# A Winograd 3x3 convolution: shorter prologue and epilogue by finer semaphores and merged weight loads

## The chip, the cores and the metric

The kernel runs on one core of a Trainium2 chip. The metric is the device time of one execution in microseconds (us), as the median of several runs. The profile adds one traced execution, whose span (first to last instruction) is 528.9 us.

## The reference

The reference is a 3x3 convolution with padding 1 over a 512 x 512 image with 96 channels in and 96 out, in bf16, written as Winograd F(2x2, 3x3):

```python
U = jnp.einsum("ar,rsck,bs->abck", G, w, G)            # transformed weights
xp = jnp.pad(x, ((0,0),(1,1),(1,1),(0,0)))
# d: all 4x4 patches of xp, two pixels apart
V = jnp.einsum("ai,ijpc,bj->abpc", Bt, d, Bt)          # transformed input
M = jnp.einsum("abck,abpc->abpk", U, V)                # products
Y = jnp.einsum("ma,abpk,nb->pmnk", At, M, At)          # back: 2x2 outputs a patch
```

The kernel uses the Winograd form along the rows only. For each pair of output rows (2t, 2t+1) it makes four combinations of input rows (a = 0 to 3), multiplies each with transformed weights, and recombines the four products into two output rows. Along the columns it keeps three taps.

## The kernel before

There are T = 256 row pairs. For each pair t:

- SyncE loads two rows of x with a transposing DMA into a ring of 8 buffers (`Xn`), so that channels lie on partitions.
- VectorE makes the four transforms of the rows (`Vt`, ring of 8).
- TensorE makes products 1 and 2 in two PSUM banks ("first half-step", 12 matmuls), and later adds products 0 and 3 into the same banks ("second half-step", 12 matmuls, `finish_pair`).
- ScalarE evacuates both banks after each half-step (one instruction of 128 x 768 for both banks), into `Ms`.
- VectorE makes the two output rows from the four evacuated tiles (`compute_y`), and GpSimd stores four rows at a time; SyncE stores the last four in two stores.

The weights, nine tiles of 96 x 96, are loaded by nine DMAs, three on each of three issuers:

```python
def load_weight(eng, sem, r, s_):
    src = bass.AP(w.tensor, w.offset + (r * 3 + s_) * C * K, [[K, C], [1, K]])
    off = r * KB + (2 - s_) * K
    eng.dma_start(Wraw[0:C, off:off + K], src).then_inc(sem, 16)

w_split = {
    "sp": [(1, 0), (1, 1), (1, 2)],
    "act": [(0, 0), (0, 1), (0, 2)],
    "pool": [(2, 0), (2, 1), (2, 2)],
}
```

```python
@block.sync
def _(sp):
    wt = _Waiter(sp)
    for (r, s_) in w_split["sp"]:
        load_weight(sp, w_sems["sp"], r, s_)
    for m in range(T):
        load_pair(sp, wt, m)              # L158: transposing load of rows 2m, 2m+1
    out_dma_pair(sp, wt, T - 2, o_last)   # L198, waits for y_cnt
    out_dma_pair(sp, wt, T - 1, o_last)
    sp.wait_ge(o_last, 32)
```

VectorE clears its borders and a tile of zeros, waits for all weights, transforms them, and then begins with x. Pairs 0 and 1 are transformed one by one (`v_single`), later pairs two at a time (`v_ops`, one instruction for two pairs):

```python
# vector engine
wait_weights(wt)
W0, W1, W2 = ...                          # rows of the 3x3 kernel, 96 x 288 each
dve.tensor_tensor(Wf1[0:C, :], W0, W2, ALU.add).then_inc(u_sem, 1)            # L325
dve.tensor_single_scalar(Wall[0:C, 0:KB], W0, 2.0, ALU.mult)
dve.tensor_single_scalar(Wall[0:C, 3 * KB:4 * KB], W2, 2.0, ALU.mult)
wt("u", u_sem, 1)
dve.tensor_tensor(Wall[0:C, 1 * KB:2 * KB], Wf1[0:C, :], W1, ALU.add)         # L329
dve.tensor_tensor(Wall[0:C, 2 * KB:3 * KB], Wf1[0:C, :], W1, ALU.subtract).then_inc(u_sem, 1)
wt("init", init_sem, 1)
compute_vgroup_part(0, 0)                 # pair 0: four v_single, L261
compute_vgroup_part(0, 1)                 # pair 1
compute_vgroup_part(1, 0)                 # pairs 2 and 3: v_ops, L279
compute_vgroup_part(1, 1)
for t in range(T):
    compute_vgroup_part(t // 2 + 2, t % 2)
    if t >= 2:
        compute_y(t - 2)                  # L318, L319
compute_y(T - 2)
compute_y(T - 1)
```

TensorE fills the time before the first data with 16 matmuls on zeros (L361):

```python
# tensor engine
wt("init", init_sem, 1)
for i in range(N_WARM):                   # 16
    pe.matmul(psets[RPS - 1][:, BANK:2 * BANK], Zt[0:C, 0:Q], Zt[0:C, 0:BANK], start=True, stop=True)
wt("u", u_sem, 2)
wait_weights(wt)
...
for t in range(T):
    conv_set(t, 1, 0, False, waits=[("vd", v_dve, vd_target(t))])    # 6 matmuls, L381
    conv_set(t, 2, 1, False).then_inc(m12_done, 1)                   # 6 matmuls
    if t >= 1:
        finish_pair(t - 1)                                           # products 0 and 3, L378
finish_pair(T - 1)
```

```python
# scalar engine
def b_evacuate(tp):
    wt("ab", ab_done, tp + 1)
    act.activation(ms2_ap(tp, 2), banks2(tp), ACT.Copy, scale=0.5).then_inc(b_evac, 1)   # L233
```

Of the kernel before, what the change touches and what calls it, by code (L numbers as in the profile page):

```python
# [5 lines left out]
ACT = mybir.ActivationFunctionType  # L6
ALU = mybir.AluOpType
# [17 lines left out]
def bass_standalone__winograd__vision_kernel(  # L25
# [23 lines left out]
    RY = 16  # L49
# [4 lines left out]
    with ExitStack() as es, nc.Block() as block:  # L54
# [25 lines left out]
        o_last = es.enter_context(nc.semaphore("o_last"))  # L80

# [51 lines left out]
        def vd_target(t):  # L133
            if t == 0:
                return 1
            return 2 * (t // 2 + 1)
# [31 lines left out]
        def load_weight(eng, sem, r, s_):  # L168
            src = bass.AP(w.tensor, w.offset + (r * 3 + s_) * C * K, [[K, C], [1, K]])
            off = r * KB + (2 - s_) * K  # L170
            eng.dma_start(Wraw[0:C, off:off + K], src).then_inc(sem, 16)  # L171

        w_split = {
            "sp": [(1, 0), (1, 1), (1, 2)],
            "act": [(0, 0), (0, 1), (0, 2)],
            "pool": [(2, 0), (2, 1), (2, 2)],
# [15 lines left out]
        def out_dma_pair(eng, wt, t, sem):  # L192
            wt("yc", y_cnt, t + 1)
            yslot = (2 * t) % RY
            src = bass.AP(YO, yslot * KY, [[RY * KY, 128], [1, 2 * KY]])
            dst = bass.AP(out.tensor, out.offset + 2 * t * orow_elems,
                          [[KY, Q], [orow_elems, 2], [1, KY]])
            eng.dma_start(dst, src).then_inc(sem, 16)  # L198
# [3 lines left out]
        @block.sync  # L202
        def _(sp):
            wt = _Waiter(sp)
            for (r, s_) in w_split["sp"]:
                load_weight(sp, w_sems["sp"], r, s_)
            for m in range(T):
                load_pair(sp, wt, m)
            out_dma_pair(sp, wt, T - 2, o_last)
            out_dma_pair(sp, wt, T - 1, o_last)  # L210
            sp.wait_ge(o_last, 32)

        @block.gpsimd
        def _(pool):
            wt = _Waiter(pool)
            for (r, s_) in w_split["pool"]:
                load_weight(pool, w_sems["pool"], r, s_)
            ng_count = [0] * NG
            for g in range(NG_POOL):
                out_dma(pool, wt, g, o_dma[g % NG])  # L220
                ng_count[g % NG] += 1
            for sg in range(NG):
                pool.wait_ge(o_dma[sg], 16 * ng_count[sg])

        @block.scalar
        def _(act):
            wt = _Waiter(act)
            for (r, s_) in w_split["act"]:
                load_weight(act, w_sems["act"], r, s_)

            def b_evacuate(tp):
                wt("ab", ab_done, tp + 1)
                act.activation(ms2_ap(tp, 2), banks2(tp), ACT.Copy, scale=0.5).then_inc(b_evac, 1)  # L233

            for t in range(T):
                wt("m12", m12_done, t + 1)
                if t >= RM:
                    wt("yc", y_cnt, t - RM + 1)
                act.activation(ms2_ap(t, 0), banks2(t), ACT.Copy, scale=0.5).then_inc(m_evac, 1)  # L239
                if t >= 1:  # L240
                    b_evacuate(t - 1)
            b_evacuate(T - 1)

        @block.vector
        def _(dve):
# [45 lines left out]
            def compute_vgroup_part(g, which):  # L291
                if g >= NGRP:
                    return
                if g == 0:
                    if which == 0:
                        for a in (1, 2, 0):
                            v_single(0, a)
                        v_single(0, 3).then_inc(v_dve, 1)
                    else:
                        for a in (1, 2, 0):  # L300
                            v_single(1, a)
                        v_single(1, 3).then_inc(v_dve, 1)
                    return
# [9 lines left out]
            def compute_y(t):  # L313
                wt("be", b_evac, t + 1)
# [3 lines left out]
                dve.tensor_tensor(yo_ap(h0), ms_ap(t, 2), ms_ap(t, 1), ALU.add)  # L318
                dve.tensor_tensor(yo_ap(h0 + 1), ms_ap(t, 0), ms_ap(t, 3), ALU.subtract).then_inc(y_cnt, 1)  # L319

            wait_weights(wt)
            W0 = Wraw[0:C, 0:KB]
            W1 = Wraw[0:C, KB:2 * KB]
            W2 = Wraw[0:C, 2 * KB:3 * KB]
            dve.tensor_tensor(Wf1[0:C, :], W0, W2, ALU.add).then_inc(u_sem, 1)  # L325
            dve.tensor_single_scalar(Wall[0:C, 0:KB], W0, 2.0, ALU.mult)
            dve.tensor_single_scalar(Wall[0:C, 3 * KB:4 * KB], W2, 2.0, ALU.mult)
            wt("u", u_sem, 1)
            dve.tensor_tensor(Wall[0:C, 1 * KB:2 * KB], Wf1[0:C, :], W1, ALU.add)  # L329
            dve.tensor_tensor(Wall[0:C, 2 * KB:3 * KB], Wf1[0:C, :], W1, ALU.subtract).then_inc(u_sem, 1)  # L330
            wt("init", init_sem, 1)
            compute_vgroup_part(0, 0)
            compute_vgroup_part(0, 1)
# [22 lines left out]
        def _(pe):  # L356
# [7 lines left out]
            wait_weights(wt)  # L364
# [19 lines left out]
            def finish_pair(tp):  # L384
                conv_set(tp, 0, 0, True, waits=[("me", m_evac, tp + 1)])
                conv_set(tp, 3, 1, True,
                         waits=[("be", b_evac, tp + 2 - RPS + 1)]).then_inc(ab_done, 1)

            assert RPS >= 3
            for t in range(T):  # L390
                conv_set(t, 1, 0, False, waits=[("vd", v_dve, vd_target(t))])
# [32 lines left out]
```

## Time and profile before

| | before |
|---|---|
| median of 6 runs | 528.38 us |
| lowest and highest | 523.74 and 539.83 us |
| span of the traced execution | 528.9 us |
| granted clock of TensorE, mean | 0.99 |
| first matmul on real data | 9.25 us |
| last matmul over | 525.0 us |

In the profile's names, PE is TensorE, DVE is VectorE, ACT is ScalarE, POOL is GpSimd and SP is SyncE; SPq is SyncE's sequencer, which issues DMAs. L158 is line 158 of the kernel. A timeline row has its start, its duration, the engine and line, what is written and read, how many instructions were merged into the row, and in brackets how long the engine stood idle before it and what released it. A row of the groups of instructions ends with the time busy, the mean duration in ns and the idle time before it. Two instructions of VectorE can overlap a little at their ends, so the distance between starts says more than the duration.

### The profile page before, as it was taken

What the parts mean: (1) busy time and instruction counts of PE and PEld (TensorE: products, weight loads), DVE (VectorE), ACT (ScalarE), POOL (GpSimd) and SP (SyncE); (2) the same over time, 40 slices, a digit from 0 to 9 for tenths busy, and PEclk for the clock granted to TensorE, in tenths of its full rate; (3) what the DMA queues carried; (4) which work ended last, traced back from release to release, by engine and by line L of the source; (5) the groups of instructions that cost most, each with busy time, mean ns of one, the idle gap of its engine ahead of it and who ended that gap; (6) DMA issues with size and microseconds to landing.
All of it is one profiled execution on the core that took longest, in us unless ns stands there. A gap on an engine that the chain in (4) does not pass through costs nothing.

```text
span 528.9 us, 14957 instructions
## 1 busy us (share of the span) xinstructions
PE 519.4 (98%) x6160; PEld 496.7 (94%) x6160; DVE 468.2 (89%) x1099; ACT 415.2 (79%) x513; POOL 97.6 (18%) x134
## 2 busy tenths in 40 slices
PE   7999999999999999999998999999999999999997
PEld 3999999999999999999998899999999999999996
DVE  5899999999999999998786889979998999999992
ACT  2688888888888888888886688878888888888886
POOL 1112112112112112121121121212121212112111
PEclk8899999999999999999999899999999999999999
DMA  7999999999999999999999999999999999999963
GB/s 141 182 258 232 214 272 239 234 233 235 225 225 230 251 207 223 236 221 232 209 180 185 246 235 255 207 218 252 253 218 248 258 257 201 251 258 232 230 164 120
DMA packets 287476, 118.60 MB, mean 224 GB/s; under 512 B 274656, under 2 KB 277248, under 8 KB 287408
## 3 DMA queue, kind: packets, MB, share of 16 engines
q1 hardware_dynamic: 272752, 67.59, 82.5%
q0 software_dynamic: 14320, 50.00, 28.8%
q8 instruction: 48, 0.79, 0.6%
q14 instruction: 20, 0.16, 0.1%
q10 hardware_dynamic: 336, 0.06, 0.1%
HBM read 0.17 MB, written 50.33 MB: 95 GB/s over the span
## 4 chain that ended last, share of the span: by engine, by line
PE 82%; DMA 10%; DVE 3%; SPq 3%; issue 1%; ACT 0%; POOL 0%; DVEq 0%; ACTq 0%; POOLq 0%
PE ps L378 41%; PE ps L381 41%; DMA Xn<-in_x_dram 9%; SPq L158 3%; DVE Vt L279 1%; DMA Wraw<-in_w_dram 1%; DVE Vt L261 1%; ACT Ms L233 0%; DVE YO L318 0%; DVE Vt L282 0%; DVE YO L319 0%; POOL Wraw L171 0%; ACT Ms L239 0%; DVE Wf L325 0%; DVE Wall L330 0%
## 5 line engine op out<-in xcount | busy, mean ns | idle before, releaser
L279 DVE TENSOR_TENSOR Vt<-Xn 96x1024 bf16<-96x1024 bf16 x445 | 288.7, 680 | 26.1 <-DMA Xn<-in_x_dram 25.8
L381 PE MATMUL ps<-Wall,Vt 96*128 96x96 bf16 (+2 forms) x3072 | 298.4, 248 | 3.6 <-DVE Vt L279 2.1
L378 PE MATMUL ps<-Wall,Vt 96*128 96x96 bf16 (+2 forms) x3072 | 297.7, 247 | 0.5 <-ACT Ms L239 0.5
L381 PEld LDWEIGHTS ps<-Wall,Vt 96*128 96x128 bf16 x3072 | 247.8, 115 | 13.2 <-DVE Vt L279 2.6
L239 ACT ACTIVATE Ms<-ps 128x768 bf16<-128x768 f32 x256 | 207.5, 810 | 62.4 <-PE ps L381 54.0
L378 PEld LDWEIGHTS ps<-Wall,Vt 96*128 96x128 bf16 x3072 | 246.7, 115 | 9.7 <-ACT Ms L239 1.2
L233 ACT ACTIVATE Ms<-ps 128x768 bf16<-128x768 f32 x256 | 207.3, 810 | 46.1 <-PE ps L378 46.0
L190 POOL DMA_DIRECT2D out_dram<-YO x127 | 95.7, 753 | 425.8 <-DVE YO L319 410.2
L318 DVE TENSOR_TENSOR YO<-Ms 128x384 bf16<-128x384 bf16 x256 | 90.3, 353 | 24.9 <-ACT Ms L233 19.8
L319 DVE TENSOR_TENSOR YO<-Ms 128x384 bf16<-128x384 bf16 x256 | 89.2, 349 | 0.0
L282 DVE TENSOR_TENSOR Vt<-Xn 96x512 bf16<-96x512 bf16 x125 | 46.9, 414 | 1.4 <-DMA Xn<-in_x_dram 1.2
L361 PE MATMUL ps<-Zt 96*128 96x512 bf16 x16 | 6.4, 588 | 1.5 <-DVE Zt L249 1.5
L361 PEld LDWEIGHTS ps<-Zt 96*128 96x128 bf16 x16 | 2.2, 142 | 5.1 <-issue 3.6
L325 DVE TENSOR_TENSOR Wf<-Wraw 96x288 f32<-96x288 bf16 x1 | 0.5, 455 | 4.9 <-DMA Wraw<-in_w_dram 4.9
L239 ACT ACT_TABLE_LOAD x1 | 1.3, 1283 | 2.1 <-issue 2.1
L261 DVE TENSOR_TENSOR Vt<-Xn 96x512 bf16<-96x512 bf16 x7 | 2.5, 411 | 0.0
L171 POOL DMA_DIRECT2D Wraw<-in_w_dram x3 | 1.7, 573 | 0.9 <-POOLq L409 0.9
L247 DVE MEMSET Vt<- 128x32 bf16 x1 | 0.1, 85 | 0.9 <-PEq L409 0.9
L330 DVE TENSOR_TENSOR Wall<-Wf,Wraw 96x288 bf16<-96x288 f32 x1 | 0.4, 448 | 0.0
L329 DVE TENSOR_TENSOR Wall<-Wf,Wraw 96x288 bf16<-96x288 f32 x1 | 0.4, 447 | 0.0
L261 DVE TENSOR_TENSOR Vt<-Zt,Xn 96x512 bf16<-96x512 bf16 x1 | 0.4, 412 | 0.0
L282 DVE TENSOR_TENSOR Vt<-Xn,Zt 96x512 bf16<-96x512 bf16 x1 | 0.4, 412 | 0.0
(8 smaller groups left out, 1.2 us busy)
## 6 DMA issues: line engine op xcount, KB each, us to landing
out_dram<-YO POOLq DMA_DIRECT2D x127, 384.0 KB, 4.9
Xn<-in_x_dram SPq DMA_TRANSPOSE x256, 5.4
out_dram<-YO SPq DMA_DIRECT2D x2, 192.0 KB, 2.0
Wraw<-in_w_dram ACTq DMA_DIRECT2D x3, 18.0 KB, 2.3
Wraw<-in_w_dram SPq DMA_DIRECT2D x3, 18.0 KB, 2.1
Wraw<-in_w_dram POOLq DMA_DIRECT2D x3, 18.0 KB, 2.8
Xn<-in_x_dram SPq DMA_DIRECT2D x1, 3.0 KB, 4.8
```

Source lines behind the costliest of these rows:

```text
L158: eng.dma_start_transpose(xpair_ap(m, 0, 2 * W), src).then_inc(x_ld[ps], 16)
L190: eng.dma_start(dst, src).then_inc(sem, 16)
L233: act.activation(ms2_ap(tp, 2), banks2(tp), ACT.Copy, scale=0.5).then_inc(b_evac, 1)
L239: act.activation(ms2_ap(t, 0), banks2(t), ACT.Copy, scale=0.5).then_inc(m_evac, 1)
L261: return dve.tensor_tensor(vtile_ap(t, a, XC0, C, 1, W), xrow_ap(r0, C), xrow_ap(r1, C), op)
L279: res.append(dve.tensor_tensor(o, in0, in1, op))
L282: res.append(dve.tensor_tensor(vtile_ap(tt, a, XC0, C, 1, W), xrow_ap(r0, C), xrow_ap(r1, C), op))
L318: dve.tensor_tensor(yo_ap(h0), ms_ap(t, 2), ms_ap(t, 1), ALU.add)
L319: dve.tensor_tensor(yo_ap(h0 + 1), ms_ap(t, 0), ms_ap(t, 3), ALU.subtract).then_inc(y_cnt, 1)
L361: pe.matmul(psets[RPS - 1][:, BANK:2 * BANK], Zt[0:C, 0:Q], Zt[0:C, 0:BANK], start=True, stop=True)
L378: ins = pe.matmul(o, lhsT, rhs, start=False, stop=(idx == n - 1), skip_group_check=True)
L381: ins = pe.matmul(o, lhsT, rhs, start=(idx == 0), stop=(idx == n - 1))
```

## The change

The change is meant to shorten both ends of the pipeline.

- Weights: three DMAs instead of nine, each with one row of the 3x3 kernel (96 x 288). ScalarE issues two and GpSimd one. SyncE issues none, and so begins with x at once. The tiles now lie in plain order, and the reversal of the column taps moves into the weight operations, which become 96 wide.
- VectorE first makes three transforms of pair 0, then waits for the weights, makes the weights of products 1 and 2, then those of 0 and 3, and then the fourth transform of pair 0 and pair 1.
- TensorE may begin pair 0 when three of its transforms and the weights of products 1 and 2 are there.
- Pairs 2 to 5 are transformed one by one, each with its own signal, instead of two at a time.
- At the end the evacuation of the last pair is split by bank, each output row of the last pair has its own signal, and the last four rows go out in three stores instead of two.

The core of the diff (declarations of three semaphores and helper definitions are cut):

```diff
-        def vd_target(t):
+        NEARLY = 6
+        def vd_target(t, full=True):
             if t == 0:
-                return 1
-            return 2 * (t // 2 + 1)
+                return 2 if full else 1
+            if t < NEARLY:
+                return t + 2
+            return NEARLY + 1 + 2 * ((t - NEARLY) // 2 + 1)
...
-        def load_weight(eng, sem, r, s_):
...
+        def load_weight(eng, sem, r):
+            src = bass.AP(w.tensor, w.offset + r * 3 * C * K, [[K, C], [C * K, 3], [1, K]])
+            dst = bass.AP(Wraw, r * KB, [[3 * KB, C], [K, 3], [1, K]])
+            eng.dma_start(dst, src).then_inc(sem, 16)
         w_split = {
-            "sp": [(1, 0), (1, 1), (1, 2)],
-            "act": [(0, 0), (0, 1), (0, 2)],
-            "pool": [(2, 0), (2, 1), (2, 2)],
+            "sp": [],
+            "act": [0, 1],
+            "pool": [2],
         }
...
         # sync engine, end
-            out_dma_pair(sp, wt, T - 2, o_last)
-            out_dma_pair(sp, wt, T - 1, o_last)
-            sp.wait_ge(o_last, 32)
+            wt("yc", y_cnt, T - 1)
+            out_dma_rows(sp, H - 4, 2, o_last)
+            wt("y0l", y0_last, 1)
+            out_dma_rows(sp, H - 2, 1, o_last)
+            wt("yc", y_cnt, T)
+            out_dma_rows(sp, H - 1, 1, o_last)
+            sp.wait_ge(o_last, 48)
...
         # scalar engine
             def b_evacuate(tp):
+                if tp == T - 1:
+                    wt("al", a_last, 1)
+                    act.activation(ms_ap(tp, 2), bank(tp, 0), ACT.Copy, scale=0.5).then_inc(ae_last, 1)
+                    wt("ab", ab_done, tp + 1)
+                    act.activation(ms_ap(tp, 3), bank(tp, 1), ACT.Copy, scale=0.5).then_inc(b_evac, 1)
+                    return
...
         # vector engine, compute_vgroup_part
                     if which == 0:
-                        for a in (1, 2, 0):
-                            v_single(0, a)
+                        v_single(0, 1)
+                        v_single(0, 2)
+                        v_single(0, 0).then_inc(v_dve, 1)
+                    else:
                         v_single(0, 3).then_inc(v_dve, 1)
-                    else:
                         for a in (1, 2, 0):
                             v_single(1, a)
                         v_single(1, 3).then_inc(v_dve, 1)
+                    return
+                if 2 * g < NEARLY:
+                    tt = 2 * g + which
+                    if which == 0:
+                        wait_vslots(g)
+                    for a in (1, 2, 0):
+                        v_single(tt, a)
+                    v_single(tt, 3).then_inc(v_dve, 1)
                     return
...
         # vector engine, weights
-            wait_weights(wt)
...
-            dve.tensor_tensor(Wf1[0:C, :], W0, W2, ALU.add).then_inc(u_sem, 1)
-            dve.tensor_single_scalar(Wall[0:C, 0:KB], W0, 2.0, ALU.mult)
-            dve.tensor_single_scalar(Wall[0:C, 3 * KB:4 * KB], W2, 2.0, ALU.mult)
-            wt("u", u_sem, 1)
-            dve.tensor_tensor(Wall[0:C, 1 * KB:2 * KB], Wf1[0:C, :], W1, ALU.add)
-            dve.tensor_tensor(Wall[0:C, 2 * KB:3 * KB], Wf1[0:C, :], W1, ALU.subtract).then_inc(u_sem, 1)
             wt("init", init_sem, 1)
             compute_vgroup_part(0, 0)
+            wait_weights(wt)
...
+            dve.tensor_tensor(Wf1[0:C, :], wraw(0), wraw(2), ALU.add).then_inc(u_sem, 1)
+            wt("u", u_sem, 1)
+            ins = None
+            for s_ in range(3):
+                dve.tensor_tensor(wall(1, s_), wf1(s_), wraw(1, s_), ALU.add)
+                ins = dve.tensor_tensor(wall(2, s_), wf1(s_), wraw(1, s_), ALU.subtract)
+            ins.then_inc(u_sem, 1)
+            for s_ in range(3):
+                dve.tensor_single_scalar(wall(0, s_), wraw(0, s_), 2.0, ALU.mult)
+                ins = dve.tensor_single_scalar(wall(3, s_), wraw(2, s_), 2.0, ALU.mult)
+            ins.then_inc(u_sem, 1)
             compute_vgroup_part(0, 1)
...
         # tensor engine
             wt("u", u_sem, 2)
-            wait_weights(wt)
...
             def finish_pair(tp):
-                conv_set(tp, 0, 0, True, waits=[("me", m_evac, tp + 1)])
+                ins0 = conv_set(tp, 0, 0, True, waits=[("me", m_evac, tp + 1), ("vd", v_dve, vd_target(tp)),
+                                                    ("u", u_sem, 3)])
+                if tp == T - 1:
+                    ins0.then_inc(a_last, 1)
...
             for t in range(T):
-                conv_set(t, 1, 0, False, waits=[("vd", v_dve, vd_target(t))])
+                conv_set(t, 1, 0, False, waits=[("vd", v_dve, vd_target(t, full=False))])
```

## The prediction

> **What bounds the kernel now.** I read the page from the top: the busy shares, the 40 slices and the groups of instructions.
>
> ```profile
> PE 519.4 (98%) x6160; PEld 496.7 (94%) x6160; DVE 468.2 (89%) x1099; ACT 415.2 (79%) x513; POOL 97.6 (18%) x134
> ...
> L279 DVE TENSOR_TENSOR Vt<-Xn 96x1024 bf16<-96x1024 bf16 x445 | 288.7, 680 | 26.1 <-DMA Xn<-in_x_dram 25.8
> ...
> L325 DVE TENSOR_TENSOR Wf<-Wraw 96x288 f32<-96x288 bf16 x1 | 0.5, 455 | 4.9 <-DMA Wraw<-in_w_dram 4.9
> ```
>
> TensorE is busy nearly always; VectorE's longest idle stretches are waits for loads of x. Next comes the chain of waits, in order of time. Here it crosses from the start into the regular rhythm:
>
> ```profile
> 10.50 2.11 PE ps L381 x12
> 12.61 1.92 PE ps L378 x12
> 14.53 1.92 PE ps L381 x12
> 16.45 1.46 PE ps L378 x12
> 17.91 0.99 PE ps L381 x12
> ```
>
> One half-step (12 matmuls: the first or the second half of a row pair) takes 0.99 us in the rhythm, so 256 pairs need 512 x 0.99 = 506.9 us. The first four half-steps after 10.50 take 7.41 us instead of 3.96: 3.45 us lost. The table by stretch of time names the reason; its last three columns are the granted clock, the DMA share and GB/s:
>
> ```profile
> 11.00:12.00 1.00, 1.00 (x9) 0.79 (x7) 1.00 (x3) 0.25 (x1) 0.00 (x0) 0.50 0.80 132
> ...
> 290.00:300.00 10.00, 7.85 (x74) 6.77 (x74) 8.36 (x21) 5.45 (x7) 1.50 (x2) 0.83 1.25 231
> ```
>
> The clock is halved from about 10.4 to 17.2 us. The second line is another loss: TensorE waits for VectorE, and that for x. From 17.91 there are 253 first and 254 second half-steps left, 501.9 us, so the last would end at 519.8; the chain has it at 525.0. The middle thus costs 5.1 us in this execution, nearly all of it between 280 and 300 us.
>
> Last the timeline at both ends:
>
> ```profile
> 2.12 29.57 SPq L158 DMA_TRANSPOSE Xn<-in_x_dram  x18
> ...
> 6.29 0.46 DVE L325 TENSOR_TENSOR Wf<-Wraw 96x288 f32<-96x288 bf16 x1 [4.89 <-DMA Wraw<-in_w_dram]
> ...
> 9.25 3.36 PE L381 MATMUL ps<-Wall,Vt 96*128 96x288 bf16 x24 [1.43 <-DVE Vt L261]
> ...
> 525.01 0.81 ACT L233 ACTIVATE Ms<-ps 128x768 bf16<-128x768 f32 x1 [0.28 <-PE ps L378]
> 525.04 0.35 DVE L319 TENSOR_TENSOR YO<-Ms 128x384 bf16<-128x384 bf16 x1
> 525.42 1.49 SPq L198 DMA_DIRECT2D out_dram<-YO  x2
> 525.86 0.36 DVE L318 TENSOR_TENSOR YO<-Ms 128x384 bf16<-128x384 bf16 x1 [0.47 <-ACT Ms L233]
> 526.13 0.35 DVE L319 TENSOR_TENSOR YO<-Ms 128x384 bf16<-128x384 bf16 x1
> ```
>
> The start is a chain on VectorE: weights land, five weight operations (to 7.69), four transforms of pair 0 (matmuls begin at 9.25), four of pair 1 (end 10.44, matmuls of pair 1 begin at 10.50). The end: matmuls stop at 525.0, evacuation, two output operations, one store, span 528.9. So the span is an account: 9.25 before the first real matmul + 506.9 of matmuls + 0.26 idle between pairs 0 and 1 (10.24 to 10.50) + 3.45 of halved clock + 5.1 in the middle + 3.9 after the last matmul = 528.9. The change can touch only the first, third and last terms, and perhaps the fourth.
>
> **What the Trainium skill says.** "TensorE: Matmul & The Clock Gate", section "Part 1: The HAM clock gate", says that the array runs at half clock until an activity window of about 3.4 us has been busy, that an idle window halves it again, and that the windows run freely and don't start with the kernel. The trace fits: the 16 warm-up matmuls come mostly every 0.427 us, the clock falls at 10.4 after idle stretches, and near 293.7 it falls for 3.4 us after a wait. "VectorE: DVE Perf Modes", section "Side-by-side: where the cycles go for N=2048 bf16", gives each instruction about 150 cycles beside its elements. The trace agrees: in the groups of instructions, 1024 elements take 680 ns and 512 take 411, so 142 ns are fixed. "DMA: Bandwidth & Descriptors", section "Issuing engines are not separate DMA queues", says that several issuers save only sequencer time, as all use the same 16 DMA engines; this bears on merging the weight loads. Here three loads on one issuer take 1.34 us to issue (0.74 to 2.08), and the first x load is issued right behind them at 2.12.
>
> **The change, part by part, at the start.**
> (1) SyncE no longer loads weights, so the x loads should begin at 0.74, not 2.12: 1.38 us earlier. The first took 4.3 us to land, so pair 0 should be there at about 5.05 (before: 6.4).
> (2) ACT issues two merged loads and GpSimd one, 54 KB each instead of 18. One load's issue took 0.40 to 0.45 us on SP and ACT, and the 192 KB stores have about the same (0.41 median), so I keep 0.45. ACT's land at about 4. GpSimd's starts at 1.30; its last small one landed 3.7 us after its issue. With more descriptors and x transfers in flight I say 3.5 to 4.5 us: 4.8 to 5.8.
> (3) VectorE does three transforms of pair 0 first. They follow each other every 0.335 us (8.69 minus 8.36 is 0.33): 5.1 to 6.1. The weights are there by then, so their wait is hidden.
> (4) The weight operations: Wf at 6.1, done at 6.57; the next one must now wait for it, since nothing independent stands between: 6.64. Then six 96-wide fp32 operations instead of two 288-wide. A 288-wide one starts 0.37 us after the other and takes 0.447 us by its group's row; with 1.04 ns an element (288 elements = 300 ns over a fixed 147) a 96-wide one comes every 0.17 us: 1.02 us against 0.74. The sixth ends near 7.8 and TensorE begins at 7.9, 1.35 us earlier than 9.25. The six scalings (0.145 us apart at 288 wide, about 0.095 at 96 wide) add 0.57: 8.23.
> (5) But TensorE only has pair 0's first half-step, to 8.86. Pair 1 waits for VectorE: the moved fourth transform of pair 0 and four of pair 1, 5 x 0.335 from 8.23, last one's end at 8.23 + 4 x 0.335 + 0.41 = 9.98. Pair 1's matmuls start at about 10.05 against 10.50. **Of the 1.35 us only 0.45 survives**, the rest becomes idle time (8.86 to 10.05) before the second half-step.
> (6) Pairs 2 to 5 go one by one: 4 x 0.335 = 1.34 us a pair where two merged ones took 2.44, 0.12 us more a pair. Pair 2 is ready at 11.3, pair 3 at 12.7; TensorE, even at full clock, asks for pair 2 at 12.0 and pair 3 at 14.0. No gain, no loss.
>
> **At the end.** The last 128x768 evacuation (0.81 us) is split by bank. The first half can start while the last six matmuls run, but ScalarE is on pair 254 until 524.73, so halves of about 0.5 us (my estimate: less than 0.81, more than half of it, as some of the 0.81 is fixed) end at 525.2 and 525.7. VectorE ends pair 254 at 525.4, does the first output row to 525.75 and the second by 526.05, against 526.49. SyncE issues three stores of about 0.42 us: 525.42, 525.85 and 526.27, so its sequencer, not the data, sets the last one: 0.22 us earlier than 526.49. That store is 96 KB, not 192; the last 192 KB moved in about 0.55 us (data flowed from 527.5 to 528.05), so 0.15 to 0.28 less. Together about 0.4.
>
> **Sum.** 0.45 + 0.4 = 0.85 us of 528.4, 0.16%: about 527.5.
>
> **The rivals.**
> (a) The whole 1.35 us (or the 1.38 of the earlier x stream) reaches the end: 526.6. Against it: VectorE's sum of work until pair 1 is ready grows from 4.15 us (6.29 to 10.44) to 4.9 (5.1 to 9.98), and pair 1 waits for all of it.
> (b) The clock: starting real matmuls at 7.9, next to the warm-up (last one over at about 7.8), could keep the clock up and save up to 3.45 us: 524. For it: the idle stretch before pair 0 goes. Against: a new one of 1.2 us comes after pair 0, so the busy share between 7 and 10.4 us hardly grows. I count 0.2 us for it.
> (c) Weights become the last wait: merged small-row loads beside transposes that start earlier, through the same DMA engines. Landing at 7 instead of 5.8 would move pair 1 to about 10.9: 528.8, a small loss.
> (d) The middle swallows it: x arrives late near 290 us, whatever the start. The stall would end at the same time if x supply alone set it, but SyncE also starts 1.38 us earlier, and the queue waits 92.4 us in all for free buffers, so the supply is mostly paced by VectorE. Then the gain at the start survives or is lost in the scatter; 527.9 if only the end counts.
>
> **Range and chances.** The known effect, about 1 us, is smaller than the scatter of the six runs, 523.74 to 539.83, which I put down to the middle stalls and the clock's window: both differ from run to run. I predict 527.3; the median of a few runs can lie 4 us off that way, so 523.3 to 531.5. Two per cent is 10.6 us, more than all idle time that the change could reach, so only scatter could give it: 0.03 faster, 0.95 same, 0.02 slower.
>
> **What would show it.** In the changed profile: the first transposing load at 0.74, pair 0's transforms from about 5.1, Wf at about 6.1 with its wait for the weights gone, first real matmul near 7.9, an idle TensorE from 8.9 to 10.0 released by VectorE, pair 1 at 10.0; 0.99 us a half-step unchanged; last matmul to span end 3.5 us, with three stores 0.42 us apart. I am wrong if Wf still waits for weights past 6.5, if the clock isn't halved after 10 us, or if waits for x in the middle grow or vanish beyond what repeated runs scatter.

## The result, and the profile after

The changed kernel takes 521.89 us (median of 8 runs, 521.73 to 524.05), beside 528.0 us for the kernel before (16 runs, 523.73 to 539.83). The ratio is 0.9908, 95% interval 0.9873 to 0.9944: faster, by less than 2%. The predicted time, 527.3, was too high, and its range (from 523.3) misses the result. Runs more than 1.5% above the fastest of their kernel (in series A to D below 43 of 242 of the kernel before, over all series 1 of 45 of the changed kernel) are left out of all ratios and of the counts of waiting runs, so both understate the longest waits; medians and ranges of device time are over all runs.

The busy shares and the groups of instructions of the changed kernel:

```profile
PE 513.9 (99%) x6160; PEld 494.5 (95%) x6160; DVE 473.8 (91%) x1115; ACT 416.5 (80%) x514; POOL 96.6 (19%) x132
...
L297 DVE TENSOR_TENSOR Vt<-Xn 96x1024 bf16<-96x1024 bf16 x437 | 282.7, 680 | 1.0 <-DMA Xn<-in_x_dram 1.0
...
L279 DVE TENSOR_TENSOR Vt<-Xn 96x512 bf16<-96x512 bf16 x23 | 7.9, 408 | 3.9 <-DMA Xn<-in_x_dram 3.9
```

The waits of VectorE's transforms of two pairs for x are 1.0 us, where the kernel before had 25.8; the 3.9 us are the wait for pair 0. The chain of waits, in order of time, shows the second difference:

```profile
10.18 1.18 PE ps L426 x12
11.37 0.99 PE ps L423 x12
12.36 0.99 PE ps L426 x12
13.35 0.99 PE ps L423 x12
```

The half-steps after pair 1's start take 0.99 us from the second on; before, the first four took 2.11, 1.92, 1.92 and 1.46. The table by stretch of time agrees (third number from the end: granted clock):

```profile
10.00:14.00 4.00, 3.82 (x47) 3.71 (x48) 4.00 (x13) 2.24 (x3) 0.00 (x0) 1.00 1.06 166
```

Last the timeline at both ends:

```profile
0.75 24.61 SPq L166 DMA_TRANSPOSE Xn<-in_x_dram  x16
...
6.31 0.45 DVE L368 TENSOR_TENSOR Wf<-Wraw 96x288 f32<-96x288 bf16 x1
...
7.95 1.18 PE L426 MATMUL ps<-Wall,Vt 96*128 96x288 bf16 x12
...
10.18 1.18 PE L426 MATMUL ps<-Wall,Vt 96*128 96x288 bf16 x12 [1.06 <-DVE Vt L279]
...
12.19 1.15 PE L426 MATMUL ps<-Wall,Vt 96*128 96x288 bf16 x12
...
514.12 2.25 PE L423 MATMUL ps<-Wall,Vt 96*128 96x288 bf16 x24
...
516.02 0.48 ACT L246 ACTIVATE Ms<-ps 128x384 bf16<-128x384 f32 x1
...
516.41 0.49 ACT L248 ACTIVATE Ms<-ps 128x384 bf16<-128x384 f32 x1
...
516.88 1.44 SPq L206 DMA_DIRECT2D out_dram<-YO  x3
517.04 0.35 DVE L351 TENSOR_TENSOR YO<-Ms 128x384 bf16<-128x384 bf16 x1
```

The start lies within 0.2 us of the prediction's points: x at 0.75, Wf at 6.31 without a wait for weights, pair 0 at 7.95, a gap of 1.06 us left by VectorE, pair 1 at 10.18. The last matmul is over at 516.37 (514.12 + 2.25), and the span ends 3.6 us later, where it was 3.9.

The account in the prediction's form: 7.95 + 506.9 of matmuls + 1.2 idle between pairs 0 and 1 + 0 of halved clock + about 0.3 for the rest + 3.6 = 520.0. What is gone beyond the predicted terms is the halved clock (3.45 us in the first trace) and the middle (5.1 us).

### The profile page after: what moved, and what is told of

The parts are those of the page before. It is cut to its first block, busy times and chain, and to the rows that moved or that the text cites. A ratio compares the mean times of both kernels' runs of the same rounds, so it can differ in the third digit from the quotient of the medians.

```text
span 520.0 us, 14966 instructions
## 1 busy us (share of the span) xinstructions
PE 513.9 (99%) x6160; PEld 494.5 (95%) x6160; DVE 473.8 (91%) x1115; ACT 416.5 (80%) x514; POOL 96.6 (19%) x132
## 4 chain that ended last, share of the span: by engine, by line
PE 97%; DVE 1%; DMA 1%; ACT 0%; issue 0%; DVEq 0%
PE ps L426 49%; PE ps L423 49%; DMA Xn<-in_x_dram 1%; DVE Vt L279 0%; ACT Ms L251 0%; DVE Wall L372 0%; DVE Wall L373 0%; DVE Wf L368 0%; DVE YO L349 0%; DVE Wall L376 0%; DVE Wall L377 0%; DVE YO L346 0%; DVEq L54 0%; DVE YO L351 0%; DVEq L21 0%
## 5 line engine op out<-in xcount | busy, mean ns | idle before, releaser
L297 DVE TENSOR_TENSOR Vt<-Xn 96x1024 bf16<-96x1024 bf16 x437 | 282.7, 680 | 1.0 <-DMA Xn<-in_x_dram 1.0
L300 DVE TENSOR_TENSOR Vt<-Xn 96x512 bf16<-96x512 bf16 x125 | 47.0, 414 | 0.2 <-DMA Xn<-in_x_dram 0.2
L279 DVE TENSOR_TENSOR Vt<-Xn 96x512 bf16<-96x512 bf16 x23 | 7.9, 408 | 3.9 <-DMA Xn<-in_x_dram 3.9
L372 DVE TENSOR_TENSOR Wall<-Wf,Wraw 96x96 bf16<-96x96 f32 x3 | 0.7, 249 | 0.0
L373 DVE TENSOR_TENSOR Wall<-Wf,Wraw 96x96 bf16<-96x96 f32 x3 | 0.7, 246 | 0.0
```

Of the source, the lines that this page charges most:

```text
L279: return dve.tensor_tensor(vtile_ap(t, a, XC0, C, 1, W), xrow_ap(r0, C), xrow_ap(r1, C), op)
L297: res.append(dve.tensor_tensor(o, in0, in1, op))
L300: res.append(dve.tensor_tensor(vtile_ap(tt, a, XC0, C, 1, W), xrow_ap(r0, C), xrow_ap(r1, C), op))
```

## The experiments

Two traces can't say which of these is the change's doing, so the experiments ask for each. Every run also gives its span and the mean granted clock of TensorE. The span is 1.8 us shorter than the device time for the kernel before, its variants, a_merged and best_hold, and 2.0 us for the changed kernel and its other variants; why isn't known, but 0.2 us of what the changed kernel gains in span is missing in device time. By the clock the runs of the kernel before fall into groups. In the first series these are 52 runs on one chip:

| mean clock | runs | typical span where x isn't waited for |
|---|---|---|
| 0.998 to 1.0 (no fall recorded at the start) | 19 | 521.1 us |
| 0.996 or 0.997 (one window of 3.4 us halved) | 14 | 521.9 us |
| up to 0.995 (two windows) | 19 | 523.4 us |

On top come waits for x, in all groups. "Waiting run" below means a run more than 1.5 us above the lowest span of its kernel; for the kernel before, above its clock group's span. Most of these runs have no trace, so that it was x they waited for is inferred. Kernels of one series ran side by side on one chip.

### Series A: clock, x loads, pairs 2 to 5

**b_warm22**: the kernel before, with a longer warm-up.

```diff
-        N_WARM = 16
+        N_WARM = 22
```

> The kernel before with 22 warm-up matmuls in place of 16, so that TensorE has less or no idle time before pair 0; nothing else is changed. Theory CLOCK (the halved clock from 10.4 to 17.2 us costs 3.45 us directly, and the waits for x in the middle follow from the state it leaves behind): clock not halved after 10 us, median about 522.7, scatter under 1 us, x issued with pauses after some 100 us. Theory XLEAD (the waits in the middle come from the x loads starting late, the clock is a separate matter): clock not halved, so about 3.4 us less, but the scatter of several us stays: median about 525, highest above 527. If the clock is halved all the same, the warm-up isn't what decides it.

Median 523.21 us against 524.93 of before; ratio 0.9989, 0.9966 to 1.0013, so no difference beyond noise by the ratio. But the clock isn't halved in any of 12 runs, and ten spans lie within 0.6 us of the lowest, 521.1. Two runs wait (524.4 and 526.5). Filling the idle time before pair 0 is enough to keep the clock; it does not end the waits. Its timeline shows what the full clock meets next in the order of the kernel before, the merged transforms of pairs 2 and 3:

```profile
13.11 1.18 PE L381 MATMUL ps<-Wall,Vt 96*128 96x288 bf16 x12 [0.66 <-DVE Vt L279]
```

Pair 2 begins at 13.11, after a wait of 0.66 us; in the changed kernel at 12.19, without one.

**b_xfirst**: the kernel before, with the x loads ahead of the weights.

```diff
-            "sp": [(1, 0), (1, 1), (1, 2)],
-            "act": [(0, 0), (0, 1), (0, 2)],
+            "sp": [],
+            "act": [(0, 0), (0, 1), (0, 2), (1, 0), (1, 1), (1, 2)],
```

> The kernel before with SyncE's three weight loads moved to ScalarE, so that the x loads begin at 0.74 us; VectorE's order and the warm-up are as before. Theory CLOCK: the clock is still halved, median within 1.5 us of before (527 to 529), scatter of several us as before. Theory XLEAD: the waits for x in the middle go, median about 524.5 (3.4 us of halved clock stay), scatter under 1.5 us.

525.86 us (524.65 to 526.98), ratio 1.0021, 1.0003 to 1.004. The six loads on ScalarE's queue land later, and pair 0 starts at 10.15, not 9.25, with the clock halved in all runs. As the weights land later too, the run doesn't tell what earlier x loads alone would bring. Device times scatter over 2.3 us, where XLEAD expected under 1.5; 3 of 10 runs wait, and the expected median of 524.5 did not come.

**a_nowarm**: the changed kernel without warm-up (`N_WARM = 0`).

> The changed kernel without any warm-up matmul, so that TensorE's clock should be halved from its first real matmul at 8 us until 11 to 18 us. Theory CLOCK: 2 to 4 us lost directly and the waits for x in the middle return: median 526 to 530, scatter of several us. Theory XLEAD: only the direct loss: median 524 to 526, scatter under 1.5 us, no waits for x after 30 us.

524.8 us (523.89 to 526.7); the lowest span is 521.9 where the changed kernel's is 519.7. A cold start costs some 2.2 us, as XLEAD expected, and only 2 of 20 runs wait. Theory CLOCK falls: a slow start does not cause the waits. The mean clock reads 0.998 to 1.0 in these runs although the trace has half-steps of 1.92 us until about 17 us: the record begins with the clock's first rise and counts the time before it as 1.00. The groups above stand all the same, as in every trace with 16 or more warm-up matmuls the clock rose by 8.1 us.

**a_merged**: the changed kernel with `NEARLY = 2`, so that pairs 2 to 5 are transformed two at a time.

> The changed kernel with pairs 2 to 5 transformed two at a time as in the kernel before (the part with NEARLY undone). Theories CLOCK and XLEAD: 521.9 plus 0.2 to 0.5 us, as pair 2 is ready at 12.4 us where TensorE asks for it at 12.2; scatter under 1 us. Rival PAIRS (one by one transforms at the start keep VectorE and x in step): the waits for x in the middle return, median 524 to 528.

522.27 us, ratio 0.9952 (0.9936 to 0.9968); 3 of 20 runs wait.

```profile
12.64 1.18 PE L426 MATMUL ps<-Wall,Vt 96*128 96x288 bf16 x12 [0.24 <-DVE Vt L297]
```

Pair 2 starts after a wait of 0.24 us, and the lowest span is 520.1 against 519.7 elsewhere: this part is worth 0.2 to 0.4 us of span at full clock, and 0.2 less in device time. Rival PAIRS is not supported.

### Series B: the idle time, and the end

**after_again**: the changed kernel itself.

> The changed kernel once more, beside the next three on one chip. In the runs so far the kernel before falls into groups by its granted clock: a span of 521.1 to 521.4 us where the clock isn't halved, about 0.7 more with one halved window of 3.4 us, about 2.2 more with two, and on top waits for x in some runs. Theory SUM (start, pair 2 and end give about 1.3 us together, the kept clock gives the rest but for the waits for x): span 519.7 to 520.1 us and a clock of 0.998 or more in nearly all runs, a wait for x in one run in ten. Rival X (the change also takes the waits for x away): none in 15 or more runs, while before has them in a fifth.

522.34 us (22 runs) against 527.34; ratio 0.9953, 0.9928 to 0.9978. The clock is 0.998 or more in all runs, the lowest span 519.8. But 8 of 22 runs wait, up to 525.2. Of before at full clock 6 of 12 do. So SUM is right on span and clock and too low on waits, and rival X is wrong: the waits are still there.

**a_oldend**: the changed kernel with the end of the kernel before.

```diff
-                if tp == T - 1:
-                    wt("al", a_last, 1)
-                    act.activation(ms_ap(tp, 2), bank(tp, 0), ACT.Copy, scale=0.5).then_inc(ae_last, 1)
-                    ...
-            out_dma_rows(sp, H - 2, 1, o_last)
-            wt("yc", y_cnt, T)
-            out_dma_rows(sp, H - 1, 1, o_last)
+            wt("yc", y_cnt, T)
+            out_dma_rows(sp, H - 2, 2, o_last)
```

> The changed kernel with the end of the kernel before (one evacuation and one store for the last pair). By the prediction's step for the end: 0.4 us more than the changed kernel, clock unchanged. Rival: under 0.15 us, if the stores' common latency hides the earlier evacuation.

522.32 us, lowest span 520.0 against 519.8, median spans 520.3 both. By the traces the end (last matmul to span end) is 3.6 us with the change and 3.9 without: 0.3, of which the medians show nothing. The change makes the last output row 0.5 us earlier after the last matmul (DVE's last row ends 1.0 us after it, not 1.5), but SyncE's three issues follow each other every 0.5 us and end 1.95 us after it, where the two old ones end at 1.9. The issues eat the earlier row; only the smaller store is left.

**a_warm13**: the changed kernel with `N_WARM = 13`.

> The changed kernel with 13 warm-up matmuls in place of 16, which ends the warm-up 0.4 to 1.3 us earlier and adds as much idle time of TensorE before pair 0, more than the kernel before had; nothing else moves. Theory IDLE (the clock falls when the idle time between warm-up and pair 1 fills about half of a window of 3.4 us; it is 1.9 us before and 1.6 after): the clock is halved in half of the runs or more, and those spans are 1 to 3.5 us longer. Rival: no run with a halved clock, if it is VectorE's order and not idle time that decides.

524.8 us, and no run below a span of 521.7: all 22 lose 1.9 us or more. In 15 of the 22 the recorded clock fell. In the traced run it did not rise until about 18 us. The timeline:

```profile
1.45 5.73 PE L407 MATMUL ps<-Zt 96*128 96x512 bf16 x13 [1.45 <-DVE Zt L267]
8.07 4.34 PE L426 MATMUL ps<-Wall,Vt 96*128 96x288 bf16 x24 [0.89 <-DVE Wall L373]
12.21 2.13 PE L423 MATMUL ps<-Wall,Vt 96*128 96x288 bf16 x12
```

Pairs 0 and 1 run at the slow rate without a gap between them. The table by stretch of time still has a clock of 1.00 there (third number from the end), as the rise had not come yet:

```profile
10.00:14.00 4.00, 3.87 (x26) 2.93 (x25) 4.00 (x13) 1.62 (x2) 0.00 (x0) 1.00 1.09 193
```

Three matmuls fewer, and the clock falls or doesn't rise in time: the warm-up of 16 has little to spare. The 15 runs fit IDLE; a warm-up too short to raise the clock at all was not in that theory.

**a_hold**: pair 0 held back within idle time that is there anyway.

```diff
-            wt("u", u_sem, 2)
+            wt("u", u_sem, 3)
+            wt("vd", v_dve, 2)
```

> The changed kernel with pair 0's matmuls held until all its four transforms and all weights are there (about 8.8 us in place of 7.9); pair 1 is due at 10.1 as before, so nothing on the path to pair 1 moves, and the idle time of TensorE between warm-up and pair 1 keeps its sum of 1.6 us. Theory IDLE: same time and clock as the changed kernel. Rival EARLY (work right behind the warm-up is what keeps the clock): clock halved in many runs, median 1 us or more longer.

523.54 us, with a wide interval (0.9921 to 1.0001). The lowest span is the same, 520.0, but the clock was halved in 3 of 13 runs, against 1 of 44 runs of the changed kernel in all series. So the sum of idle time isn't all; where it lies matters too (see the clock below). IDLE in its strict form fails, and EARLY holds only for some runs.

### Series C: the lead of the x loads, and another order

**a_xlate**: the changed kernel, x loads from the sixth on delayed by three loads that nobody reads.

```diff
             for m in range(T):
                 load_pair(sp, wt, m)
+                if m == 4:
+                    for i in range(3):
+                        src = bass.AP(w.tensor, w.offset + i * C * K, [[K, C], [1, K]])
+                        sp.dma_start(Wdum[0:C, i * K:(i + 1) * K], src).then_inc(d_sem, 16)
```

> The changed kernel, but after its fifth x load SyncE issues three small loads that nobody reads, which delays all later x loads by about 1.35 us, as much as the kernel before begins them later; pair 5 then lands about 2 us before it is needed, so nothing waits at the start. Theory XLEAD (waits for x in the middle depend on how far the x loads are ahead before the stores begin): as many and as long waits as in the kernel before, so the median is 1 to 4 us over the changed kernel's 522, and scatter like before's. Rival: same time as the changed kernel, median 521.8 to 522.6; then the earlier x stream isn't what makes the waits rarer.

525.43 us (522.02 to 535.96) against 526.25; the lowest span is 520.0 as ever, and 10 of 16 runs wait. The start is untouched (pair 1 at 9.84, no early wait), so the 1.5 us of SyncE, if they cost anything, are paid only later, and not in every run. The changed kernel did not run beside it.

**b_xfirst_again**: b_xfirst once more.

> The kernel before with only the x loads moved ahead of the weights, once more, with more repeats and a chip of its own. Theory XLEAD: the lower half of its runs lies at 525 to 526 (span 523.1 to 524.5, halved clock as before), but few runs lie more than 2 us above; on a chip where the kernel before has many waits, it is faster than before by 1 us or more. Rival: as many runs with waits as before, so at or above before's median.

526.09 us, ratio 1.0014 (0.999 to 1.0038). Of 14 runs one lies far up (span 528.2), the rest within 2.1 us of the lowest, 523.3: few long waits, as XLEAD says. The gain of 1 us that XLEAD expected did not come: it loses at the start (pair 0 at 10.83 in its trace).

**a_lead32**: the changed kernel with `N_WARM = 32`, which holds TensorE back.

> The changed kernel with 32 warm-up matmuls in place of 16, which hold TensorE back: pair 1 starts at about 12 us and not 10.1, with no idle time before it. Theory XLEAD: 1.9 us are lost at the start, but x gets 1.9 us further ahead, so that hardly any run waits for x: span 521.6 to 522.2 in nine runs of ten. Rival: as many runs with waits as the changed kernel (over a third had more than 1 us on the last chip).

524.04 us, ratio 0.9973 (0.9953 to 0.9993); lowest span 521.3; 4 of 21 runs wait, against 10 of 16 of a_xlate beside it. XLEAD had expected nine of ten within 522.2 and got 13 of 21. The edit also leaves TensorE no idle time before pair 1, so lead isn't all that it changes.

**best**: another order on VectorE, by TensorE's need. `v_half` is a signal of its own for the first half-step of pairs 0 to 3.

```diff
-            compute_vgroup_part(0, 0)
+            v_single(0, 1)
+            v_single(0, 2).then_inc(v_half, 1)
             wait_weights(wt)
...          # weights of products 1 and 2
+            v_single(1, 1)
+            v_single(1, 2).then_inc(v_half, 1)
...          # scalings
-            compute_vgroup_part(0, 1)
-            compute_vgroup_part(1, 0)
-            compute_vgroup_part(1, 1)
+            for tp in range(NHALF):              # NHALF = 4
+                v_single(tp, 0)
+                v_single(tp, 3).then_inc(v_dve, 2 if tp == 0 else 1)
+                if tp + 2 < NHALF:
+                    v_single(tp + 2, 1)
+                    v_single(tp + 2, 2).then_inc(v_half, 1)
```

> The changed kernel with VectorE's first operations put in the order in which TensorE needs them: for pairs 0 to 3 the two transforms of the first half-step get a signal of their own, those of pair 1 come before the scalings of the weights, the other transforms after. TensorE should start pair 0 at 7.6, pair 1 at 8.6 in place of 10.1, with no idle time. Theory SUM: 1.3 us faster than the changed kernel where no run waits for x (span about 518.6). Theory XLEAD: x is 1.3 us less ahead, so more runs wait for x than with the changed kernel, and the median gains less.

522.39 us (521.0 to 530.55) against 526.25; ratio 0.9941, 0.9903 to 0.998. The timeline has pairs 0 and 1 back to back:

```profile
7.78 2.14 PE L434 MATMUL ps<-Wall,Vt 96*128 96x288 bf16 x24
...
9.93 1.15 PE L431 MATMUL ps<-Wall,Vt 96*128 96x288 bf16 x12
```

The lowest span, 519.0, is 0.7 under the changed kernel's lowest, 519.7 (1.3 were expected); 4 of 10 runs wait. In its trace the second half-step of pair 0 begins 1.27 us earlier than in the changed kernel's, but TensorE then stands until 18.29 behind ScalarE, which waits for VectorE's output rows, and 0.44 us are lost again. It beats the kernel before. Against the changed kernel it wasn't run side by side, and the waits are larger than the difference.

### Series D: with the changed kernel beside them

**after_third**

> The changed kernel, as the measure for the next three on the same chip: span 519.7 to 520.3 where it doesn't wait for x, clock 0.998 or more, waits of over 1.5 us in a quarter of the runs at most.

523.62 us (14 runs) against 525.59; ratio 0.9972, 0.9939 to 1.0005. Lowest span 519.9, but 7 of 13 runs wait, twice the expected share and more than the 13 of 52 of the kernel before. The interval reaches past 1, so this series alone doesn't show the changed kernel to be faster.

**a_xlate_again**: a_xlate once more.

> The changed kernel with the x loads from the sixth on delayed by three small loads (1.5 us of SyncE), once more, now with the changed kernel beside it. Theory XLEAD: same lowest spans (520.0) and clock as the changed kernel, but waits of over 1.5 us in half of the runs or more, median 1.5 us or more above the changed kernel's. Rival (the last chip alone made them): median within 0.7 us of the changed kernel's.

524.76 us, ratio 1.0002 (0.9977 to 1.0027), 1.1 us above the changed kernel; 14 of 18 runs wait against its 7 of 13. The direction is XLEAD's, the size is between the two theories, and the intervals overlap, so it isn't shown.

**b_xfirst_warm**: the kernel before with b_xfirst's edit and `N_WARM = 26`.

> The kernel before with two things alone: x loads ahead of the weights (weights moved to ScalarE), and 26 warm-up matmuls, so that TensorE is hardly idle before pair 0. VectorE's order, pairs 2 to 5 and the end are as before. Weights land later than before (6.3 to 6.6 us in the earlier run of the x loads alone), so its start is 0.9 to 1.5 us later than before's. Theory SUM with XLEAD: clock never halved, spans of 521.9 to 522.8, few waits; so it has the gain of the clock and of the waits, and lacks the direct 1.3 us and the later weights. Rival: waits as in before.

526.0 us, ratio 1.0018 (0.9993 to 1.0044). Its lowest span is 521.9, as expected, but the clock fell in 8 of 22 runs, as pair 0 starts at 11.05 and 26 matmuls leave 1.4 us of idle time; and 7 of the 14 runs with a full clock wait. So it doesn't show that both parts alone bring the gain, and its waits speak against lead as the only cause.

**best_hold**: best, with the first stores held back and a larger output ring.

```diff
-    RY = 16
+    RY = 32
-            wt("yc", y_cnt, 2 * g + 2)
+            wt("yc", y_cnt, max(2 * g + 2, 11 + (7 * g + 4) // 5))
```

> The changed kernel with VectorE's order by need (as in the run best) and with the first stores held back: a ring of 32 output rows in place of 16, the first store after pair 10, the next ones a little faster than the pairs until they have caught up at group 15. Theory XLEAD: the x ring fills before the stores compete, so spans of 518.6 to 519.2 in nine runs of ten, median 3 us under before's cleanest. Rival: the later stores crowd the loads all the same, and waits of several us come in a third of the runs.

527.65 us, 13 of 16 runs wait: the rival was right. The rows of the x loads between 40 and 60 us (issue: min, median, max in ns; then the time to landing), in best_hold's profile:

```profile
L168 SPq DMA_TRANSPOSE Xn<-in_x_dram x9: 1357/1958/4412, 39.7 to 58.6; - x9
DMA to landing us min/median/max: 5.3/8.7/10.5
```

and in the changed kernel's:

```profile
L166 SPq DMA_TRANSPOSE Xn<-in_x_dram x11: 1304/1650/3176, 39.7 to 58.3; - x11
DMA to landing us min/median/max: 3.7/5.6/7.5
```

In that stretch best_hold issues 7 stores instead of 6, having issued 2 instead of 6 in the 20 us before. With slightly denser stores the median landing is 8.7 in place of 5.6 us, and 9 loads are issued in place of 11. That the stores are the reason is argued: it is one trace of each, and the order on VectorE differs too.

### Series E: lead down and up

**a_xlate6**: a_xlate with six loads in place of three.

> The changed kernel with the x loads from the sixth on delayed by six small loads, about 3 us of SyncE's time; pair 5 then lands at about 15 us, still before TensorE asks for it at 16.2. Theory XLEAD, sharpened: a loss of lead costs more later than a loss at the start. Lowest spans still about 520.0, but median 524 us or more, and above that of a_lead32b beside it, although the latter loses 1.9 us at the start. Rival: median about 522.5, below a_lead32b.

527.34 us, ratio 1.0045 (1.0022 to 1.0069). The lowest span is 523.2, not 520.0: VectorE now waits for x so early that its output rows come late, and TensorE waits 1.2 us at 20 us behind ScalarE. This run lost at the start too, and the clock fell in 15 of the 20 runs, so it tells less than it was meant to. 12 of 20 runs wait beyond that.

**a_lead32b**: a_lead32 once more.

> The changed kernel with 32 warm-up matmuls once more: TensorE begins pair 1 some 1.9 us later, so the x loads are 1.9 us further ahead. Theory XLEAD: lowest span 521.3, four of five runs within 1.5 us of it, median 523.2 to 524.2, below that of a_xlate6. Rival: waits as often as in a_xlate6, so median 1.5 us or more above it.

524.11 us, ratio 0.9974 (0.9949 to 0.9998); lowest span 521.1, 4 of 22 runs wait, and four more lie just at the limit. The order of the medians is XLEAD's, with the reservation above.

The lists of waits of single traces don't settle it. The largest of VectorE's waits for x behind the start (total, times, longest) in a_xlate_again, in after_third and in a_lead32:

```profile
DVE Vt L304 <- DMA Xn<-in_x_dram: 13.7, 17, 1.7
...
DVE Vt L297 <- DMA Xn<-in_x_dram: 8.8, 14, 1.6
...
DVE Vt L297 <- DMA Xn<-in_x_dram: 7.9, 11, 1.7
```

In a_lead32b only the wait for pair 0 is left:

```profile
DVE Vt L279 <- DMA Xn<-in_x_dram: 3.9, 1, 3.9
```

But the spans of these four are 520.4, 520.0, 523.4 and 522.6. In the first two TensorE waits for nothing behind pair 1: waits of VectorE cost time only when TensorE comes to wait too. In the last nothing is lost behind the start at 11.64 (522.6 - 11.64 = 510.9; the changed kernel's 520.0 - 7.95 - 1.24 of idle time is 510.8), so its 1.5 us over the lowest span lie in the start (32 warm-up matmuls end later when the clock rises later), not in waits for x.

Over all series:

| x loads relative to the changed kernel | kernels | waiting runs |
|---|---|---|
| 1.9 us further ahead | a_lead32, a_lead32b | 8 of 43 |
| as they are | the changed kernel, three times; a_oldend | 19 of 65 |
| 1.5 us less ahead | a_xlate, a_xlate_again | 24 of 34 |

The series had different chips, so the table is no clean comparison; the two within one series (4 of 21 against 10 of 16 in C, 7 of 13 against 14 of 18 in D) go the same way, the second within chance. The same start gave 8 of 22 (after_again) and 3 of 21 (a_oldend) side by side, so more lead than the changed kernel has is not shown to help; less lead goes with more waiting runs. The kernel before has a weak sign of it within itself: a halved clock holds TensorE back by 2 us, and in series A to D 19 of 82 runs with two halved windows wait, but 25 of 59 with the full clock (44 of 107 and 38 of 72 if the longest runs are counted).

## Why the prediction was wrong, point by point

**The start, steps (1) to (5): right.** x at 0.75, weights hidden, pair 1 at 10.18 (predicted 10.05): 0.32 us gained where 0.45 was predicted.

**Step (6), "No gain, no loss": wrong.** It compared the new order with TensorE's needs in the changed kernel, and forgot to ask what the old order would do at full clock: there pair 2 waits (0.66 us in b_warm22). Undoing it alone costs 0.2 to 0.4 us of span.

**The end: 0.3 by the traces, where 0.4 was predicted.** The step that failed is "0.22 us earlier" for the last issue: three issues 0.5 us apart, not 0.42, end no earlier than two.

**The sum of direct gains**: at full clock and without waits, spans of 521.1 before and 519.8 after, 1.3 us instead of 0.85 (1.1 in device time). In series D the lowest spans are 521.1 and 519.9, in B 521.6 and 519.8. The traces of b_warm22 (521.2) and of the changed kernel (520.0) show where it lies: pair 2 begins 0.92 us earlier (13.11 and 12.19), and the end is 0.3 shorter.

**Rival (b), the clock, "I count 0.2 us for it": the first term that was mis-sized.** The step that failed is "the busy share between 7 and 10.4 us hardly grows". It grew across the line at which the clock falls. The clock's rise shows in the traces where warm-up matmuls begin to follow each other every 0.21 us in place of 0.43; in the kernel before that is at 7.05. Of the 3.41 us from there TensorE is idle for 1.82 (with 0.21 us for the last warm-up matmul): 1.59 before pair 0 and 0.23 before pair 1. That is 53%, and at 10.47 the clock falls. So the stretch needn't be idle as a whole, as the prediction read it. In the three traces of the changed kernel it is idle for 1.1 to 1.4 us of that stretch, at most 40%, and the clock stays up, in 43 of 44 runs. The other traces agree: it fell at 55 and 66% (b_xfirst_again, b_xfirst), and stayed at up to 46% (b_xfirst_warm). The sum isn't what counts: after_third stayed up with 2.4 us of idle time, 1.1 and 1.3 in two stretches that follow each other. When the clock rises differs from run to run (5.2 to 8.1 us in the traces), and with it what falls into the stretch; this fits the kernel before, in which some runs keep the clock, and a_hold, whose idle time lies in one piece, but for both that is argued.

Before, the clock falls in two thirds to four fifths of the runs; with 0.8 and 2.3 us for the groups (table above), and their counts in series A, B and D (19, 14, 19; 12, 17, 20; 11, 19, 22), that averages 1.1 to 1.3 us a run. a_warm13, b_warm22 and a_nowarm show that the warm-up's reach decides it.

**Rival (d), the middle: the second, and the largest in the first comparison.** The prediction left 5.1 us of waits for x in place, as if they belonged to every run. In the first comparison, 6.1 us between medians (4.8 by the ratio), about 3.8 (2.5) are left after 1.1 and 1.2. But the changed kernel isn't rid of these waits: they came back in 8 of 22 and 7 of 13 runs, and with them the ratio was 0.9953 and 0.9972, 2.5 and 1.5 us. The direct gains and the clock, 2.3 us together, lie within both intervals, so what came back needs no fewer waits. Less lead of the x loads goes with more of them (table above), and the change hardly moves that lead: the loads start 1.38 us earlier, but TensorE also gets to pair 2 up to 0.9 us earlier and no longer loses time to a slow clock. Why the waits were rare in the 8 runs of the first comparison and many in the kernel before beside them stays open; the share differed between series for one and the same kernel, on the same chip too (10 of 52 and 20 of 46 runs of before in series A and C).

So the range failed: it was laid around the median of the kernel before, with its waits and its halved clock in it, while the changed kernel's clean run, 519.7 us of span or 521.7 of device time, lies below the range's lower end. How far the first comparison missed was in part the luck of 8 runs nearly without waits: the same kernel's median in series D, 523.62, lies inside the range.

## What to carry to other kernels

Split a kernel's runs by granted clock before pricing a change at its start: here some 0.5 us less idle time within the 3.4 us after the clock's rise kept the clock up, which on average was worth as much as all direct gains. Count idle time stretch by stretch, not as a sum. Where an engine off the critical path waits for loads, ask whether the critical one waits too before calling it a cost. Predict the clean run and the waits apart, with a range for each.

## What the runs showed of the hardware

- In the kernel before the clock stayed halved for 6.8 us from 10.5, with matmuls back to back after 10.5; after its fall at 293.8 it rose again after 3.4 us.
- Over all traces the clock fell at the start where TensorE was idle for 53 to 66% of the 3.41 us after the clock's rise, and never where it was idle for 46% or less of such a stretch.
- The recorded clock reads 1.00 before the clock's first rise, while half-steps take 1.92 us (a_nowarm, a_warm13).
- One issue of a plain load on ScalarE's queue took about as long for the merged 54 KB load as for 18 KB: two took 0.90 us, three small ones 1.38. On GpSimd the merged one took 0.80 us, a small one 0.53.
- The issue of a transposing load took 1.16 us at the least and 4.94 at the most in the kernel before. It grew along with the landing (medians of 1.65 and 5.6 us between 40 and 60 us in the changed kernel, 1.96 and 8.7 in best_hold).
